# Fetching a and b from ScalarE's own queue, with their constants planned from the first microseconds

## The chip, the core and the metric

The kernel runs on one core of a Trainium2 chip. A core has a matrix engine (TensorE, PE in the rows; its weight loads are PEld), a vector engine (VectorE, DVE), an engine for activations and copies (ScalarE, ACT), a general engine (GpSimd, POOL) and SyncE (SP), which here only issues DMAs. Each engine works through its own queue in order and waits on semaphores for the others. The metric is the device time of one execution in microseconds; lower is better. The notation x4 at the end of a row means four instructions.

## The reference, cut to what matters

```python
def sm_attn(qq, kk, vv):
    s = scale * np.matmul(qq, kk.transpose(0, 1, 3, 2))
    s = s - np.max(s, axis=-1, keepdims=True)
    a = np.exp(s)
    a = a / (np.sum(a, axis=-1, keepdims=True) + 1e-09)
    return np.matmul(a, vv)
p_packed = sm_attn(p, k, v)              # 32 packed queries
x = sm_attn(q, p_packed, p_packed)       # 8 batches, 8 heads, 576 tokens, 64 per head
...
h = x @ w_in                             # 4608 x 512 by 512 x 2048
P = a[0] + a[1] * h + a[2] * h2 + a[3] * h3      # h2 = h * h, h3 = h2 * h
Q = 1.0 + np.abs(b[0]) * np.abs(h) + np.abs(b[1]) * h2
return (P / (Q + 1e-6)) @ w_out          # 2048 x 512
```

q, k, v and p are float32; the weights, a and b come as the kernel's inputs in DRAM. a has four numbers and b two.

## The kernel before, in words

The eight batches are worked on one after the other. For a batch, `attention` loads keys, values and queries in their natural layout, transposes them (the first batches on TensorE with a copy by ScalarE into the tile KX), and makes the packed attention: scores of p against k, an exponential, the product with v, normalised on VectorE into pT and transposed into PPT. The second attention follows: scores of PPT against the queries, transposed by VectorE back into KX, then a softmax over 32 keys in two halves (maximum, subtraction, exponential on ScalarE, sum, a reciprocal, a product), and a last transpose of each half into AH (and a rest AL from the second batch on). A softmax half thus goes VectorE, ScalarE, VectorE, and TensorE's hidden matmuls wait for both halves of AH.

The FFN is cut into units: a batch, one half of its tokens, and one of eight column blocks of w_in. Per batch `m_chunk` multiplies the packed values into w_in (tile m), so `hidden` of a unit is a matmul of AH with m into the PSUM tile h. Then come U (ScalarE, the absolute value times b0), sq (ScalarE, the square times b1's root), Y (ScalarE, a3*h + a2), two VectorE steps, a sum on GpSimd, a logarithm and an exponential in place of the division, and VectorE steps that leave the unit's result in gh and gl, and its remainder rows in G. These last steps read the unit's h for the last time; there are two h tiles, so the matmuls of a unit wait for the end of the unit two before it. Three units later `acc_block` multiplies gh and gl by w_out into the PSUM tile acc. Weights come as 64-bit words and are turned into float32 by `convert`: two ScalarE passes per block and three or four steps on VectorE or GpSimd; blocks of w_in and w_out wait for that in the tiles m, w, half.

Nearly all instructions are only recorded by `Planner`. It prices each, works out the dependencies, tries several list schedules, and issues the instructions in the order of the best one's start times (`issue`, line 293 for all instructions that it issues, so the tiles tell them apart). The planner's own DMAs all go to SP's queue. Where the plan leaves TensorE idle in the first 150 us, `idle` puts filler matmuls (line 290: columns of zeros added to an open PSUM sum, which change nothing) into the gap. The first instructions, before `nc.pin()`, are DMAs whose order is fixed.

The constants are made by `constants`, which is recorded right after the pinned DMAs: two DMAs bring a and b to all 128 partitions (tile ab); VectorE scales them into abS; a chain of VectorE steps, a logarithm and an exponential on ScalarE, and three more VectorE steps make the square root of b1 in the tile root and write it to abS. ScalarE then loads a3, b0 and the root into registers (TENSOR_LOAD rows) for its activations U, sq and Y. In the plan these steps come ready when ab's DMAs do.

Of the kernel before, what the change touches and what calls it, by code (L numbers as in the profile page):

```python
# [13 lines left out]
F32 = mybir.dt.float32  # L14
# [10 lines left out]
P = 128  # L25
# [7 lines left out]
class Planner:  # L33
# [8 lines left out]
    TRANSPOSE, F32 = (15, 0.734), (30, 1.62)  # L42
# [19 lines left out]
    SWITCH = 95  # L62
    SLACK = 60, 100, 150, 220, 300
    IN_FLIGHT = 8
    DMA_ISSUE, DMA_START, DMA_END = 420, 1400, 1200

    DMA_RATE = 100.0, 190.0, 370.0
# [90 lines left out]
    def edges(self):  # L158
# [32 lines left out]
            edges.append(before)  # L191
        return edges

    def schedule(self, before, after, rank, back=0):

        n = len(rank)
        need = [len(x) for x in before]
        at, start, end = [0.0] * n, [0.0] * n, [0.0] * n
        soon = {e: [] for e in self.ENGINES}
        ready = {e: [] for e in self.ENGINES}  # L200
# [2 lines left out]
        mode, landed, dma = None, [], 0.0  # L203
        for i in range(n):
            if not need[i]:
                heapq.heappush(soon[self.ops[i][0]], (0.0, rank[i], i))
        now = 0.0
        left = n
        while left:
            for e in self.ENGINES:  # L210
                while soon[e] and soon[e][0][0] <= now:
                    heapq.heappush(ready[e], heapq.heappop(soon[e])[1:])
                if free[e] > now or not ready[e]:
                    continue
                if e == "sync" and not back and len(landed) >= self.IN_FLIGHT and landed[-self.IN_FLIGHT] > now:
                    free[e] = landed[-self.IN_FLIGHT]
                    continue
                _, i = heapq.heappop(ready[e])
# [106 lines left out]
def attention_rational_ffn(  # L325
# [38 lines left out]

    sb = ctx.enter_context(tc.tile_pool(name="sb", bufs=1))
    ps = ctx.enter_context(tc.tile_pool(name="ps", bufs=1, space=PSUM))
    tc.nc.scalar.preload_act_table_set("natural_log_exp_and_others")
    nc = Planner(tc.nc)


    ident = sb.tile([P, P], F32, name="ident")
    make_identity(tc.nc, ident)
    ab, abS, one, root = (sb.tile([P, n], F32, name=x) for n, x in ((8, "ab"), (7, "abS"), (1, "one"), (5, "root")))
    ab, eps, minus = ab[:, 0:6], ab[:, 6:7], ab[:, 7:8]
    zero = sb.tile([P, 32], F32R, name="zero")
    win = sb.tile([P, NCH, NCC, CF], F32, name="win")
    G = sb.tile([P, NFC, 2 * REM], F32, name="G")
# [25 lines left out]
    def constants():  # L403
        nc.gpsimd.memset(eps, 1e-9)
        nc.gpsimd.memset(minus, -SCALE)
        nc.vector.tensor_scalar(zero, ident[:, 0:32], 0.0, None, ALU.mult)
        nc.sync.dma_start(ab[:, 0:4], a.rearrange("(o n) -> o n", o=1).broadcast_to([P, 4]))
        nc.sync.dma_start(ab[:, 4:6], b.rearrange("(o n) -> o n", o=1).broadcast_to([P, 2]))
        nc.vector.tensor_scalar(abS[:, 0:6], ab, S, None, ALU.mult)
        nc.vector.scalar_tensor_tensor(abS[:, 4:6], abS[:, 4:6], -1.0, abS[:, 4:6], ALU.mult, ALU.max)  # L410
        nc.vector.memset(one, (1.0 + 1e-6) * S)

        m, e, p, r, i = (root[:, n : n + 1] for n in range(5))
        nc.vector.scalar_tensor_tensor(m, ab[:, 5:6], -1.0, ab[:, 5:6], ALU.mult, ALU.max)
        nc.vector.tensor_scalar(m, m, 2.0**-126, None, ALU.max)
        nc.vector.tensor_scalar(e.bitcast(I32), m.bitcast(I32), 23, None, ALU.logical_shift_right)
        nc.vector.tensor_scalar(e.bitcast(I32), e.bitcast(I32), 127, None, ALU.add)
        nc.vector.tensor_scalar(p.bitcast(I32), e.bitcast(I32), 1, 23, ALU.logical_shift_right, ALU.logical_shift_left)
        nc.vector.reciprocal(i, p)
        nc.vector.tensor_scalar(m, m, i, i, ALU.mult, ALU.mult)  # L420
        nc.scalar.activation(r, m, AF.Ln)
        nc.scalar.activation(r, r, AF.Exp, scale=0.5)
        nc.vector.reciprocal(i, r)
        nc.vector.scalar_tensor_tensor(r, m, i, r, ALU.mult, ALU.add)
        nc.vector.tensor_scalar(abS[:, 6:7], r, p, 0.5 * S**0.5, ALU.mult, ALU.mult)
        for i, reg in enumerate((reg_a3, reg_b0, reg_b1, reg_root)):
            nc.scalar.reg_load(reg, abS[0:1, 3 + i : 4 + i].bitcast(I32))
# [576 lines left out]
    for what in ("k0", "k1", "r", "p", "qr", 2, "rv", "v0", "v1", 3, "q0", "q1", 4, 5):  # L1004
        if isinstance(what, int):
            load_words(what)
        else:
            load(0, what)
    nc.pin()
    constants()  # L1010
    for _ in attention(0):
        pass
# [17 lines left out]
    for bb in range(1, B):  # L1030
        gen = attention(bb)
        at = [u for u in range(2 * UB * bb - 30, 2 * UB * bb - 3) if u not in mt]
# [89 lines left out]
```

## Time and profile before

| what | value |
|---|---|
| time, median of 3 runs (lowest to highest) | 765.78 us (765.69 to 766.87) |
| the profiled execution | 766.86 us, of which its span is 765.1 us |
| busy, share of the span: PE, DVE, ACT, POOL | 96%, 86%, 81%, 61% |
| mean granted clock of TensorE | 0.983 of 2.4 GHz |
| DMA, busy share of 16 engines, first four fortieths of the span | 0.9, 0.9, 0.9, 0.4 |

A busy time counts all of an instruction's span; matmuls are pipelined, and their ends are modelled. "Idle before" is the time in which an engine stood still ahead of an instruction, with what released it. The granted clock is TensorE's: 1.00 is 2.4 GHz, 0.50 is 1.2 GHz.

### The profile page before, as it was taken

How to read it: one execution, taken by the hardware profiler on the slowest of the kernel's cores; microseconds unless marked ns; L12 is line 12 of the kernel's file. 1: busy time of each engine (PE TensorE's matmuls, PEld its weight loads, DVE VectorE, ACT ScalarE, POOL GpSimd, SP SyncE). 2: the span in 40 equal slices, each digit the busy share in tenths (PEclk: the TensorE clock that was granted, in tenths of full speed). 3: DMA queues.
4: the chain of work that ended last, by engine and by line, in shares of the span. 5: the costliest groups of instructions: out<-in, count | busy, mean ns of one | idle time of the engine just before them, and what ended most of it. 6: DMA issues, size and time to landing. Idle time of an engine off the chain costs nothing.

```text
span 765.1 us, 14505 instructions
## 1 busy us (share of the span) xinstructions
PE 737.9 (96%) x5358; PEld 569.2 (74%) x5358; DVE 656.0 (86%) x1050; ACT 619.1 (81%) x1074; POOL 467.4 (61%) x457
## 2 busy tenths in 40 slices
PE   3689999999999999999999999999999999999997
PEld 2455645678788887778788887778788887778886
DVE  2789999898988889998998789998998889988773
ACT  6689986898786888888786888888786887887882
POOL 0026556987685566856685565955685655866672
PEclk8679999999999999999999999999999999999999
DMA  9994650203801128024701119222801016000001
GB/s 253 292 371 129 164 135 0 83 26 50 120 1 56 43 32 126 10 84 55 112 1 57 36 24 126 25 84 32 116 14 56 27 24 83 1 28 1 29 1 41
DMA packets 156630, 56.38 MB, mean 74 GB/s; under 512 B 126864, under 2 KB 145808, under 8 KB 156560
## 3 DMA queue, kind: packets, MB, share of 16 engines
q1 hardware_dynamic: 156560, 55.46, 32.8%
q8 instruction: 42, 0.69, 0.4%
q14 instruction: 28, 0.23, 0.1%
HBM read 46.01 MB, written 9.44 MB: 72 GB/s over the span
## 4 chain that ended last, share of the span: by engine, by line
PE 89%; DMA 4%; ACT 2%; DVE 2%; POOL 1%; SPq 1%; issue 1%; DVEq 0%; POOLq 0%; ACTq 0%
PE acc L293 46%; PE h L293 28%; PE at L293 15%; DMA m<-in_moe_w_in_dram 2%; PE acc L290 1%; DMA pn<-in_p_dram 1%; DVE Y L293 1%; SPq L293 1%; DMA AH<-in_k_dram 1%; ACT sq L293 0%; ACT U L293 0%; POOL U L293 0%; POOL gl L293 0%; ACT h L293 0%; ACT Y L293 0%
## 5 line engine op out<-in xcount | busy, mean ns | idle before, releaser
L293 POOL TENSOR_TENSOR U<-U,sq 128x576 f32<-128x576 f32 x128 | 185.3, 1448 | 140.9 <-ACT sq L293 135.7
L293 DVE SCALAR_TENSOR_TENSOR Y<-Y,abS,h 128x576 f32<-128x576 f32 x256 | 205.7, 804 | 55.0 <-ACT h L293 52.9
L293 PE MATMUL acc<-w,gh 128*128 128x512 f32 x736 | 240.8, 407 | 0.5 <-ACT half L293 0.5
L293 PE MATMUL h<-AH,m 128*128 128x288 f32 x1024 | 195.6, 315 | 1.7 <-DVE AH L293 1.0
L293 PEld LDWEIGHTS h<-AH,m 128*128 128x128 f32 x1024 | 159.2, 189 | 30.8 <-DVE Y L293 7.5
L293 POOL TENSOR_TENSOR gl<-Y,gh 128x512 fp32r<-128x512 f32 x116 | 150.2, 1296 | 31.2 <-POOL G L293 13.5
L293 PEld LDWEIGHTS acc<-w,gh 128*128 128x128 f32 x736 | 133.9, 188 | 45.6 <-issue 16.4
L293 PE MATMUL acc<-w,gl 128*128 128x512 f32 x384 | 150.6, 412 | 0.0
L293 ACT ACTIVATE sq<-U,one 128x576 f32<-128x576 f32 x128 | 101.1, 790 | 34.9 <-POOL U L293 34.7
L293 ACT ACTIVATE U<-h 128x576 f32<-128x576 f32 x128 | 83.3, 651 | 40.3 <-PE h L293 39.6
L293 DVE TENSOR_TENSOR Y<-Y,h 128x576 f32<-128x576 f32 x128 | 95.3, 745 | 16.0 <-ACT Y L293 15.7
L293 ACT ACTIVATE h<-sq 128x576 f32<-128x576 f32 x128 | 84.8, 663 | 21.6 <-DVE Y L293 20.0
L293 PE MATMUL h<-AL,m 128*128 128x288 f32 x448 | 97.0, 296 | 0.0
L293 ACT ACTIVATE Y<-h,abS 128x576 f32<-128x576 f32 x128 | 96.5, 754 | 0.0
L293 DVE SCALAR_TENSOR_TENSOR h<-U,h 128x576 f32<-128x576 f32 x128 | 95.9, 749 | 0.0
L293 PEld LDWEIGHTS acc<-w,gl 128*128 128x128 f32 x384 | 71.8, 188 | 22.9 <-issue 10.2
L293 DVE SCALAR_TENSOR_TENSOR Y<-h,Y 128x576 f32<-128x576 f32 x116 | 87.0, 750 | 1.9
L293 ACT CAST gh<-Y 128x512 fp32r<-128x512 f32 x116 | 73.0, 629 | 14.8 <-DVE Y L293 10.1
L293 ACT ACTIVATE sq<-h 128x576 f32<-128x576 f32 x128 | 83.5, 653 | 0.0
L293 PE MATMUL acc<-half,gh 128*128 128x512 f32 x240 | 78.2, 409 | 0.2 <-ACT gh L293 0.2
L293 PEld LDWEIGHTS h<-AL,m 128*128 128x128 f32 x448 | 71.9, 188 | 2.0 <-issue 1.4
L293 PEld LDWEIGHTS acc<-half,gh 128*128 128x128 f32 x240 | 43.9, 188 | 13.5 <-issue 5.1
(145 smaller groups left out, 904.3 us busy)
## 6 DMA issues: line engine op xcount, KB each, us to landing
w<-in_moe_w_out_dram SPq DMA_DIRECT2D x16, 512.0 KB, 5.1
out_dram<-half SPq DMA_DIRECT2D x15, 512.0 KB, 3.0
nat<-in_k_dram SPq DMA_DIRECT2D x48, 144.0 KB, 4.3
nat<-in_q_dram SPq DMA_DIRECT2D x48, 144.0 KB, 4.4
nat<-in_v_dram SPq DMA_DIRECT2D x24, 256.0 KB, 3.3
m<-in_moe_w_in_dram SPq DMA_DIRECT2D x10, 512.0 KB, 8.9
w<-in_moe_w_in_dram SPq DMA_DIRECT2D x6, 512.0 KB, 8.2
nat<-in_k_dram SPq DMA_DIRECT2D x4, 512.0 KB, 7.1
```

The costliest lines, as they stand in the source:

```text
L290: getattr(self.nc.tensor, name)(*args, **kwargs)
L293: getattr(getattr(self.nc, engine), name)(*args, **kwargs)
```

## The change

The two DMAs that bring a and b are issued from ScalarE's queue, ahead of the load of its activation table and outside the planner. The planner no longer sees a DMA that writes ab; instead an instruction that reads the tile ab and has no other dependency comes ready at 4500 ns of its schedule (`LANDED`), and not at 0. Only the forward schedule uses it. Everything behind is planned anew.

```diff
+    LANDED = 4500.0
...
+    def ready(self, calls):
+        return self.LANDED * any(isinstance(x, bass.AP) and x.tensor.name == "ab" for _, args, _ in calls for x in args)
...
             if not need[i]:
-                heapq.heappush(soon[self.ops[i][0]], (0.0, rank[i], i))
+                at[i] = 0.0 if back else self.ready(self.ops[i][1])
+                heapq.heappush(soon[self.ops[i][0]], (at[i], rank[i], i))
...
+    tc.nc.scalar.dma_start(ab[:, 0:4], a.rearrange("(o n) -> o n", o=1).broadcast_to([P, 4]))
+    tc.nc.scalar.dma_start(ab[:, 4:6], b.rearrange("(o n) -> o n", o=1).broadcast_to([P, 2]))
     tc.nc.scalar.preload_act_table_set("natural_log_exp_and_others")
...
-        nc.sync.dma_start(ab[:, 0:4], a.rearrange("(o n) -> o n", o=1).broadcast_to([P, 4]))
-        nc.sync.dma_start(ab[:, 4:6], b.rearrange("(o n) -> o n", o=1).broadcast_to([P, 2]))
```

The seven added lines move the lines behind them: 290 and 293 of before are 296 and 299 in the changed kernel.

ScalarE's first instructions, before:

```order
L1118 UNCONDITIONAL_BRANCH
L367 ACT_TABLE_LOAD
L293 COPY kx_1_87<-at_1_89 128x512
L293 COPY kx_1_87<-acc_1_90 128x512
L293 COPY kx_1_87<-acc_2_91 128x512
L293 COPY kx_1_87<-at_2_92 128x512
```

and in the changed kernel:

```order
L1124 UNCONDITIONAL_BRANCH
L375 DMA ab<-in_moe_a_dram 128x4
L376 DMA ab<-in_moe_b_dram 128x2
L377 ACT_TABLE_LOAD
L299 TENSOR_LOAD abS x2
L299 ACTIVATE root<-root 128x1 x2
L299 TENSOR_LOAD abS
L299 COPY kx_1_89<-at_1_91 128x512
L299 COPY kx_1_89<-acc_1_92 128x512
```

The first batch's copies of transposed keys (kx) now stand behind all constants; before, the constants stood some 40 rows later, between the copies into m.

VectorE in the first batch's second softmax, from the product of the first half to just ahead of the second transpose into AH, before (m_4 and win are a w_in block in conversion, w_3 and w_8 one of w_out):

```order
L293 TENSOR_TENSOR kx_1_87<-kx_1_87,small 128x576
L293 TENSOR_SCALAR root<-root 128x1
L293 STREAM_TRANSPOSE AH_3_114<-kx_1_87 128x576
L293 TENSOR_REDUCE small<-kx_1_87 128x18
L293 RECIPROCAL root<-root 128x1
L293 TENSOR_SCALAR m_4_85<-m_4_85 128x1024
L293 TENSOR_SCALAR small<-small,ab 128x18
L293 SCALAR_TENSOR_TENSOR root<-root 128x1
L293 RECIPROCAL small<-small 128x18
L293 ISA win<-m_4_85,win 128x2048
L293 TENSOR_TENSOR kx_1_87<-kx_1_87,small 128x576
L293 TENSOR_SCALAR abS<-root 128x1
```

and in the changed kernel, from the conversion of that w_in block on:

```order
L299 TENSOR_SCALAR m_4_87<-m_4_87 128x1024
L299 RECIPROCAL small<-small 128x18
L299 ISA win<-m_4_87,win 128x2048
L299 TENSOR_REDUCE small<-kx_1_89 128x18
L299 TENSOR_TENSOR kx_1_89<-kx_1_89,small 128x576
L299 TENSOR_SCALAR small<-small,ab 128x18
L299 STREAM_TRANSPOSE AH_3_116<-kx_1_89 128x576
L299 RECIPROCAL small<-small 128x18
L299 TENSOR_SCALAR w_8_134<-w_3_88 128x1024
L299 TENSOR_TENSOR kx_1_89<-kx_1_89,small 128x576
L299 TENSOR_SCALAR w_3_88<-w_3_88 128x1024
L299 STREAM_TRANSPOSE AH_3_116<-kx_1_89 128x576
```

The steps on root and abS are gone from here; the w_in block's conversion has moved ahead of the first transpose into AH, and two steps of a w_out block ahead of the second.

TensorE around the hidden matmuls of the seventh unit (h_7), before (rows with zero are fillers; at_34 with small is the packed values' transpose):

```order
L293 MATMUL at_35_195<-rv_2_110,small 32x64
L290 MATMUL acc_14_167<-half_1_157,zero 32x96 x14
L293 MATMUL at_34_194<-ident,small 128x128
L290 MATMUL acc_14_167<-half_1_157,zero 32x96 x2
L293 MATMUL h_7_190<-AH_3_114,m_7_134 128x288 x4
L293 MATMUL at_34_194<-ident,small 128x128
L290 MATMUL acc_14_167<-half_1_157,zero 32x96 x6
L293 MATMUL h_8_204<-AH_3_114,m_7_134 128x288
```

and in the changed kernel:

```order
L299 MATMUL acc_14_169<-half_1_159,gh_2_173 128x512
L296 MATMUL acc_14_169<-half_1_159,zero 32x96 x5
L299 MATMUL at_38_211<-ident,nat_7_198 128x128 x3
L299 MATMUL h_7_192<-AH_3_116,m_7_136 128x288 x4
L299 MATMUL at_38_211<-ident,nat_7_198 128x128
L299 MATMUL acc_13_168<-half_2_180,gl_2_183 128x512 x2
L299 MATMUL acc_14_169<-half_2_180,gl_2_183 128x512
L299 MATMUL h_8_206<-AH_3_116,m_7_136 128x288 x4
```

The packed values of the second batch have moved ahead of h_7, query transposes and output matmuls of the fourth unit stand around it, and of 22 fillers five are left. Over the whole kernel the order lists 41 fillers of 96 columns before, and 30 of 96 and three of 256 columns after. The last 70 or so rows of TensorE, VectorE, ScalarE and GpSimd stand in the same order in both kernels, as do the last 54 DMAs of SP's queue.

## Rows read from the trace of the kernel before

**Rows 1.** The page, busy times: engine, us (share of span) x instructions.

```profile
PE 737.9 (96%) x5358; PEld 569.2 (74%) x5358; DVE 656.0 (86%) x1050; ACT 619.1 (81%) x1074; POOL 467.4 (61%) x457
```

**Rows 2.** The page, chain that ended last: shares by engine.

```profile
PE 89%; DMA 4%; ACT 2%; DVE 2%; POOL 1%; SPq 1%; issue 1%; DVEq 0%; POOLq 0%; ACTq 0%
```

**Rows 3.** Windows: stretch, length; busy us by engine; clock, DMA share, GB/s.

```profile
38.25:42.25 4.00, 4.00 (x8) 2.72 (x9) 4.00 (x10) 0.40 (x4) 0.00 (x0) 0.50 1.00 381
60.00:84.00 24.00, 24.00 (x222) 15.48 (x221) 23.90 (x47) 23.80 (x39) 11.31 (x6) 1.00 0.43 136
150.00:600.00 450.00, 449.50 (x3398) 359.12 (x3397) 401.40 (x634) 371.11 (x653) 300.76 (x302) 1.00 0.32 57
```

**Rows 4.** Timeline, the first 10 us: start, us, instruction [idle before <- releaser].

```profile
0.73 0.98 SPq L293 DMA_DIRECT2D nat<-in_k_dram  x2
0.73 1.28 ACT L367 ACT_TABLE_LOAD   x1 [0.73 <-PEq L1107]
...
4.83 1.08 PE L293 MATMUL at<-ident,nat 128*128 128x128 f32 x4 [4.83 <-DMA nat<-in_k_dram]
...
5.95 0.58 ACT L293 COPY kx<-at 128x512 f32<-128x512 f32 x1 [3.93 <-PE at L293]
...
9.10 0.37 ACT L293 COPY small<-acc 128x256 f32<-128x256 f32 x1
```

**Rows 5.** Timeline, 20 to 24 us.

```profile
20.89 1.92 PE L293 MATMUL acc<-w,kx 128*32 128x64 f32 x60 [0.97 <-DMA w<-in_v_dram]
22.21 1.05 SPq L293 DMA_DIRECT2D ab<-in_moe_b_dram  x1
...
23.59 0.33 SPq L293 DMA_DIRECT2D ab<-in_moe_a_dram  x1
23.66 1.15 ACT L293 ACTIVATE m<-m 128x1024 f32<-128x1024 f32 x1 [4.28 <-DMA m<-in_moe_w_in_dram]
```

**Rows 6.** DMA: the queue (packets, MB, share of 16 engines), issues (KB, us to landing).

```profile
q1 hardware_dynamic: 156560, 55.46, 32.8%
...
out_dram<-full SPq DMA_DIRECT2D x16, 64.0 KB, 1.7
...
ab<-in_moe_b_dram SPq DMA_DIRECT2D x1, 1.0 KB, 10.4
```

**Rows 7.** Timeline, 38 to 45 us.

```profile
38.25 4.21 PE L293 MATMUL h<-AH,m 128*128 128x288 f32 x8 [0.96 <-DVE AH L293]
...
41.59 0.21 DVE L293 TENSOR_SCALAR abS<-root 128x1 f32<-128x1 f32 x1
41.71 0.77 DVE L293 STREAM_TRANSPOSE AH<-kx 128x576 f32<-128x576 f32 x1
...
42.23 1.19 ACT L293 ACTIVATE w<-w 128x1024 f32<-128x1024 f32 x1 [3.60 <-DVE abS L293]
...
42.41 1.47 DVE L293 TENSOR_SCALAR w<-w 128x1024 uint16<-128x1024 uint16 x2
...
43.91 1.22 DVE L293 CUSTOM_DVE_ANT_0 w<-w,w 128x2048 uint16<-128x2048 uint16 x1
...
44.47 0.65 ACT L293 ACTIVATE U<-h 128x576 f32<-128x576 f32 x1
```

**Rows 8.** Timeline, 48 to 85 us, and one group of the page (busy, mean ns).

```profile
48.98 1.98 PE L293 MATMUL at<-ident,nat 128*128 128x128 f32 x8 [2.98 <-ACT m L293]
...
65.56 0.68 PE L290 MATMUL acc<-w,zero 128*32 128x96 f32 x6
...
66.17 2.21 PE L293 MATMUL h<-AH,m 128*128 128x288 f32 x8
...
79.61 2.22 ACT L293 ACTIVATE w<-w 128x1024 f32<-128x1024 f32 x2
...
82.27 0.67 DVE L293 SCALAR_TENSOR_TENSOR gl<-h,Y 128x512 f32<-128x512 f32 x1
...
84.03 0.72 ACT L293 ACTIVATE U<-h 128x576 f32<-128x576 f32 x1
...
L293 PE MATMUL acc<-w,gh 128*128 128x512 f32 x736 | 240.8, 407 | 0.5 <-ACT half L293 0.5
```

More of the change, by code (lines that the diff above doesn't have):

```diff
@@ L366, in attention_rational_ffn @@
     ps = ctx.enter_context(tc.tile_pool(name="ps", bufs=1, space=PSUM))
+    ab, abS, one, root = (sb.tile([P, n], F32, name=x) for n, x in ((8, "ab"), (7, "abS"), (1, "one"), (5, "root")))
+    ab, eps, minus = ab[:, 0:6], ab[:, 6:7], ab[:, 7:8]
+    tc.nc.scalar.dma_start(ab[:, 0:4], a.rearrange("(o n) -> o n", o=1).broadcast_to([P, 4]))
+    tc.nc.scalar.dma_start(ab[:, 4:6], b.rearrange("(o n) -> o n", o=1).broadcast_to([P, 2]))
     tc.nc.scalar.preload_act_table_set("natural_log_exp_and_others")
@@ L372, in attention_rational_ffn @@
     make_identity(tc.nc, ident)
-    ab, abS, one, root = (sb.tile([P, n], F32, name=x) for n, x in ((8, "ab"), (7, "abS"), (1, "one"), (5, "root")))
-    ab, eps, minus = ab[:, 0:6], ab[:, 6:7], ab[:, 7:8]
     zero = sb.tile([P, 32], F32R, name="zero")
```

## The prediction

> **What bounds the kernel now.** I read the busy times and the chain of waits first. TensorE is busy 737.9 of 765.1 us [rows 1], and 89% of the chain that ended last is TensorE's [rows 2]. By windows it loses 0.5 us between 150 and 600 us [rows 3], so the end is set by when the gap-free stretch begins, by the real matmuls that are left, and by the filler matmuls that stand among them. For this kernel I write: span = real matmuls + fillers + idle TensorE. The reals are the same in both kernels, so only two terms can move: the fillers, and the idle time, which is 765.1 - 737.9 = 27.2 us and lies nearly all before 55 us. What holds TensorE there is read from the timeline: first DMA (it starts on the first keys at 4.83 us, and waits for the values at 20.89 us; ScalarE waits 4.28 us for a block of w_in until 23.66 us [rows 4, 5]), then VectorE's softmax, which ends in the two transposes into AH, then ScalarE and VectorE together (23.8 and 23.9 of 24 us busy from 60 to 84 us [rows 3]).
>
> **The fetch.** Two issues leave SP's queue at 22.21 and 23.59 us (1.05 and 0.33 us [rows 5]) and stand ahead of the table load on ScalarE, which took 1.28 us from 0.73 us [rows 4]. At SP's own durations the table load ends at 0.73 + 1.38 + 1.28 = 3.4 us, before ScalarE's first copy at 5.95 us: cost 0. The transfers are 256 tiny packets. SP's queue moved 156560 packets in 32.8% of 16 engines' 765.1 us [rows 6], 0.41 us of all engines for 256. Until 22 us the DMA engines were the limit, so the values, the w_in blocks and the queries land later by 0 to 0.4 us; I take 0.4. Afterwards those packets are gone from the queue, but ScalarE and VectorE have already been set back, so I keep it as a shift.
>
> The Trainium skill ("DMA: Bandwidth & Descriptors", section "Issuing engines are not separate DMA queues") says that DMAs started by any engine run on the same 16 DMA engines, and another issuer saves only the time to issue. That speaks against the change: by it the 0.4 us is only moved, and 1.4 us of SP's issue time is the whole gain of the fetch. If ScalarE's queue had engines of its own, the 0.4 would be 0. No row of before has two issuers.
>
> **The constants at the head.** The order pieces on ScalarE show it: three register loads and two activations now stand in front of the first copy, and the order lists VectorE's twelve small operations likewise in front of its first reduction. So the copy at 5.95 us [rows 4] waits for a and b. Their landing is not in this trace for an empty queue: the quickest transfer took 1.7 us, this one in the full queue 10.4 us [rows 6], the first keys, issued at the same time, 4.83 - 0.73 = 4.1 us [rows 4]. I take 4.1, near the row with the same moment: landed at 0.8 + 4.1 = 4.9 us (bounds 2.5 and 11.2). Then twelve dependent steps (seven on VectorE, two activations, three on VectorE) at 0.21 us, the row of the last one [rows 7], are 2.5 us, and after that last one ScalarE went on 42.23 - 41.80 = 0.43 us later [rows 7]: ready at 7.8 us. The first copy comes 1.9 us late. The four copies ran with gaps; packed at 0.58 us [rows 4] the fifth, of the packed queries' projections, starts at 7.8 + 4 x 0.58 = 10.1 instead of 9.10 us [rows 4]. That is 1.0 us late, and hidden: ScalarE next idles 4.28 us until 23.66 us, and TensorE waits for the values until 20.89 us [rows 5]. Cost 0; the cover is gone when a and b land 3.3 us later still, after about 8.2 us.
>
> The register loads: after the last constant ScalarE lost 0.43 us with the load in it [rows 7]. The Trainium skill (same page, section "Latency and other measured facts") gives a tensor_load a floor of about 0.6 us; three in series would make the constants ready some 1.4 us later, which the same idle time still hides.
>
> **The stall that goes.** ScalarE waited 3.60 us for the last constant until 42.23 us [rows 7]. Behind that wait stood one weight conversion and two copies, done by the time U of the first unit started at 44.47 us, and U's matmuls set that start (TensorE ran at a granted clock of 0.50, 1.2 GHz, from 38.25 to 42.25 us [rows 3]). In the new order ScalarE has nothing more in front of that U, so it will wait for TensorE instead: worth 0 by itself.
>
> **VectorE's softmax (the order pieces on VectorE).** Eleven small operations leave the stretch; the last one moved its successor by 41.71 - 41.59 = 0.12 us [rows 7]; at 0.1 us each, 1.1 us is saved. But the two passes over a w_out block (1.47 us [rows 7]) now stand ahead of the second transpose into AH, and the conversion of a w_in block ahead of the first. Net, the second AH comes 1.5 - 1.1 = 0.4 us later, and the first about 2 us later, while four plus four transposes on TensorE go ahead of the hidden matmuls. Those took 4.21 us at half clock [rows 7]; if the clock returns as early as before, nothing is lost, if it returns 2 us later, 1.1 us. So U of the first unit shifts by 0.4 (DMA) + 0 to 1.1; I take 0.9 in all. From there ScalarE's queue is full, and the shift is handed on: idle TensorE +0.9 us.
>
> **Fillers.** The order lists 41 filler matmuls of 96 columns before; after, 30, and three of 256 columns. The three at 65.56 us, six instructions in the trace, took 66.17 - 65.56 = 0.61 us [rows 8], 0.20 each: -2.2 us. The wide ones lie between 0 and half of a 512-column one (0.41 us [rows 8]); 0.1 each: +0.3. Sum -1.9 us. It is a gain only if TensorE has real work ready there. One place speaks for it: before the seventh unit two conversions (2.22 us [rows 8]) have moved behind that unit's U, and two short copies in front, and the 22 fillers around the seventh unit's matmuls have become five (the order pieces on TensorE).
>
> **Sum.** -1.9 + 0.9 = -1.0 us. The profiled execution took 766.86 us (1.8 around its span), so 765.9 for it; the median of the runs shown is 1.1 lower, 765.78, so 764.8.
>
> **Rivals.**
> - *Full gain*: the clock returns early, U comes no later, and the 2.98 us for which TensorE waited until 48.98 us [rows 8] shrink by about half, since the copy it waited for moved ahead of two activations. -1.9 - 1.5 = -3.4, 762.4 us. Against it: the matmuls that follow need constants of other engines at 52 us as before. Chance 0.25.
> - *Nothing moves*: the fillers only stood in time that stays idle, and the shift is made up. 765.8 us, 0.1.
> - *VectorE becomes the bound at the eighth unit* (slower): in the new order a w_out block's two passes less one (0.74 us) and its last step (1.22 us [rows 7]) stand ahead of the gl that ends at 82.27 + 0.67 us [rows 8], on an engine 23.9 of 24 us busy [rows 3]. gl and its small partner are the last readers of the PSUM buffer that the eighth unit's matmuls take. +2.0 on top of the 0.9: TensorE idle +2.9 instead of +0.9, sum +1.0, and up to +2.0 if the fillers come back as idle time; 767.3 us. It decides when that buffer comes free after TensorE's own work ahead. Against it: 2.7 us of real matmuls have moved in front of that place. Chance 0.15.
> - *a and b land late* (slower): at 10.4 us, as in SP's queue, they are there at 11.2 and the fifth copy 7.3 us late, 3.0 beyond the 4.28: 764.8 + 3.0 = 767.8 us. Against it: nothing stands ahead of them in ScalarE's queue. The Trainium skill (same page, section "Queues, rings and completion order") says that each DMA engine takes turns between the queues; by that they don't wait behind the keys. Chance 0.1.
>
> **How the numbers follow.** The forecast case, 764.8, has 0.4 and spans 763.3 to 766.3 (its 0 to 1.5 of shift, fillers -1.5 to -2.2). About 0.2% is what a measurement of this kernel tells from no change, 1.5 us. Faster by more than that: a third of the forecast case, nearly all of the full gain: 0.13 + 0.24 = 0.38 with a little of "nothing moves". Slower: 0.02 of the forecast case, two thirds of the VectorE case, most of the late landing: 0.02 + 0.1 + 0.09 = 0.21. Within: 0.41. The range for 8 in 10 reaches to the full gain below and to the late landing above: 762.0 to 768.0.
>
> **What would show it.** Right: ScalarE's first copy near 7.8 us and the fifth near 10; the ScalarE wait until 23.66 us shorter by about 1 us, the values' matmuls at 20.9 to 21.3 us; no wait of 3.6 us near 42 us but one on TensorE; the first U at 44.9 to 46 us; the seventh U earlier than 84.03 us [rows 8]; fewer fillers and less than 1 us of new waits behind 84 us. Wrong: a or b landing after 8 us, waits of TensorE on VectorE between 80 and 90 us, or new TensorE gaps after 150 us.

## The result: slower by 1%

The changed kernel takes 774.95 us (773.15 to 776.1), the kernel before, beside it, 766.33 (765.69 to 768.6): 1.010 times as long, with a 95% interval of 1.008 to 1.012. Its profiled execution took 773.15 us with a span of 771.1; TensorE's mean granted clock is 0.981. The forecast, 764.8 us, has the wrong sign.

First the page of the changed kernel, busy times and the chain that ended last, against [rows 1, 2].

```profile
PE 741.2 (96%) x5339; PEld 568.8 (74%) x5339; DVE 660.8 (86%) x1050; ACT 618.1 (80%) x1074; POOL 465.6 (60%) x457
...
PE 65%; DVE 12%; ACT 9%; issue 5%; DMA 4%; POOL 3%; SPq 1%; DVEq 0%; ACTq 0%; POOLq 0%
```

TensorE is as full as before, but the chain that sets the end is TensorE's for 65% instead of 89%: it now passes through VectorE, ScalarE and GpSimd. By the sum that the prediction used, idle TensorE grew from 27.2 to 771.1 - 741.2 = 29.9 us, and its busy time from 737.9 to 741.2 although fillers left.

Next the first 12 us of the changed kernel, the counterpart of [rows 4]: TensorE's first matmul, then ScalarE with its own DMA issues.

```profile
5.91 1.09 PE L299 MATMUL at<-ident,nat 128*128 128x128 f32 x4 [5.91 <-DMA nat<-in_k_dram]
```

```profile
0.73 0.43 ACTq L375 DMA_DIRECT2D ab<-in_moe_a_dram  x1
1.19 0.45 ACTq L376 DMA_DIRECT2D ab<-in_moe_b_dram  x1
1.67 1.28 ACT L377 ACT_TABLE_LOAD   x1 [1.67 <-PEq L1113]
7.87 0.44 ACT L299 ACTIVATE root<-root 128x1 f32<-128x1 f32 x2 [4.92 <-DVE root L299]
9.39 0.58 ACT L299 COPY kx<-at 128x512 f32<-128x512 f32 x1 [1.08 <-PE acc L299]
...
11.30 0.42 ACT L299 COPY small<-acc 128x256 f32<-128x256 f32 x1
```

And its DMA queues with the landing times of ab (last column), against [rows 6].

```profile
q1 hardware_dynamic: 156272, 55.46, 34.0%
...
q10 hardware_dynamic: 288, 0.00, 0.0%
...
ab<-in_moe_a_dram ACTq DMA_DIRECT2D x1, 2.0 KB, 3.6
ab<-in_moe_b_dram ACTq DMA_DIRECT2D x1, 1.0 KB, 5.2
```

The keys land at 5.91 instead of 4.83 us. The second of the two fetches lands 1.19 + 5.2 = 6.4 us after the start, and VectorE's first constant follows it; the copies come 3.4 us later than before, and the fifth 2.2. ScalarE around the first U, against [rows 5, 7]:

```profile
24.41 1.15 ACT L299 ACTIVATE m<-m 128x1024 f32<-128x1024 f32 x1 [2.38 <-DMA m<-in_moe_w_in_dram]
...
42.95 1.19 ACT L299 ACTIVATE w<-w 128x1024 f32<-128x1024 f32 x1 [3.91 <-DMA w<-in_moe_w_out_dram]
...
44.96 0.66 ACT L299 ACTIVATE U<-h 128x576 f32<-128x576 f32 x1
```

The 4.28 us of idle time at 24 us shrank to 2.38, so the late copies were hidden, as forecast. The stall of 3.60 us is gone, and a wait of 3.91 us for a block of w_out stands at its place. The first U starts 44.96 - 44.47 = 0.49 us late. So far nothing has happened that would make 6 us. That comes behind it: the third U starts 1.6 us late (57.57 against 56.01), the fourth 4.2 (62.98 against 58.75), the eighth 1.8, the 24th 6.0. TensorE in that stretch in the changed kernel:

```profile
48.19 0.66 PE L299 MATMUL at<-ident,nat 128*128 128x128 f32 x4 [1.79 <-ACT m L299]
50.33 1.12 PE L299 MATMUL at<-ident,nat 128*128 128x128 f32 x4 [1.48 <-ACT m L299]
...
53.29 1.11 PE L299 MATMUL at<-kx,small 64*32 64x256 f32 x16 [0.46 <-ACT small L299]
54.33 3.20 PE L299 MATMUL h<-AH,m 128*128 128x288 f32 x8
```

and the third unit's hidden matmuls and those scores before:

```profile
53.45 2.10 PE L293 MATMUL h<-AH,m 128*128 128x288 f32 x8
55.48 0.66 PE L293 MATMUL at<-kx,small 64*32 64x256 f32 x16
```

Scores of the second batch's packed attention (at<-kx,small) stand ahead of the third unit's hidden matmuls, where before they stood behind, and the eight hidden matmuls take 3.20 us where they took 2.10. Windows of the changed kernel (columns as in [rows 3]):

```profile
50.00:55.00 5.00, 4.21 (x28) 2.62 (x29) 4.40 (x9) 4.95 (x9) 0.00 (x0) 0.50 1.06 325
55.00:60.00 5.00, 5.00 (x24) 3.26 (x23) 4.10 (x7) 3.17 (x5) 1.16 (x1) 0.86 1.06 348
60.00:84.00 24.00, 22.63 (x198) 12.45 (x197) 23.00 (x44) 22.66 (x40) 9.52 (x7) 1.00 0.38 120
150.00:600.00 450.00, 447.92 (x3364) 357.81 (x3364) 403.75 (x638) 368.73 (x650) 301.83 (x303) 1.00 0.35 57
```

and the first two of these stretches before:

```profile
50.00:55.00 5.00, 4.97 (x19) 3.67 (x20) 4.32 (x8) 4.88 (x9) 0.00 (x0) 0.72 1.04 391
55.00:60.00 5.00, 5.00 (x39) 2.70 (x38) 3.62 (x9) 5.00 (x9) 3.77 (x2) 1.00 0.91 263
```

Behind its gaps at 48 and 50 us TensorE had a granted clock of 0.50, the lower of its two levels (1.2 GHz), from 50 to 55 us, where before it was 0.72. From 60 to 84 us it lost 1.4 us where it had lost nothing, and from 150 to 600 us 2.1 us against 0.5 [rows 3].

A late U is not yet a loss, since the new order puts other work between the units. A better count is TensorE's real work: every matmul that is no filler counts with the mean time that its kind took in before at the full clock, and the question is how much later the changed kernel has done as much as before. This is an estimate worked out from the two traces, good to about 0.5 us; e1, below, comes out at 0.8 to 1.2 us late from 45 to 740 us. The changed kernel is 0.4 us late at 45 us, 3.8 at 65, 0.3 at 85, 0.5 at 105, 3.8 at 153 and 6.4 at 700. So what the opening loses is won back by 85 us, and the loss that stays comes behind 105 us. The fillers have a part in both. From 60 to 92 and from 113 to 150 us (PE busy, PEld busy, clock, DMA share, GB/s), before:

```profile
60.00:92.00 32.00, 6.24 (x62) 4.95 (x62) 1.00 0.49 144
113.00:150.00 37.00, 1.84 (x20) 1.62 (x20) 1.00 0.10 29
```

and in the changed kernel:

```profile
60.00:92.00 32.00, 2.03 (x20) 1.59 (x20) 1.00 0.44 138
113.00:150.00 37.00, 3.86 (x40) 3.22 (x40) 1.00 0.07 19
```

4.2 us of fillers have left the first stretch, and 2.0 us have come into the second.

One sentence of the text on the change has to be corrected. It says that an instruction that reads the tile ab comes ready at 4500 ns. The changed kernel compares the tensor's name with "ab", and the real name carries a number behind it, so the comparison never holds and the planner believes the constants ready at 0. That is why they stand ahead of all key copies (e3, below).

### The profile page after: what moved, and what is told of

The parts are those of the page before. It is cut to its first block, busy times and chain, and to the rows that moved or that the text cites. A ratio compares the mean times of both kernels' runs of the same rounds, so it can differ in the third digit from the quotient of the medians.

```text
span 771.1 us, 14483 instructions
## 1 busy us (share of the span) xinstructions
PE 741.2 (96%) x5339; PEld 568.8 (74%) x5339; DVE 660.8 (86%) x1050; ACT 618.1 (80%) x1074; POOL 465.6 (60%) x457
## 4 chain that ended last, share of the span: by engine, by line
PE 65%; DVE 12%; ACT 9%; issue 5%; DMA 4%; POOL 3%; SPq 1%; DVEq 0%; ACTq 0%; POOLq 0%
PE acc L299 33%; PE h L299 20%; PE at L299 12%; DVE Y L299 6%; DMA AH<-in_k_dram 3%; ACT sq L299 2%; DVE small L299 2%; DVE h L299 2%; DVE kx L299 2%; ACT kx L299 1%; ACT h L299 1%; POOL U L299 1%; ACT U L299 1%; SPq L299 1%; DMA w<-in_q_dram 1%
## 5 line engine op out<-in xcount | busy, mean ns | idle before, releaser
L299 PEld LDWEIGHTS acc<-w,gh 128*128 128x128 f32 x736 | 134.0, 188 | 49.4 <-issue 16.3
```

Of the source, the lines that this page charges most:

```text
L299: getattr(getattr(self.nc, engine), name)(*args, **kwargs)
```

## The experiments

Three kinds of edit were used. In the first, a kernel makes both plans, the one of before (its two DMAs of ab planned on SP's queue but not issued) and the one of the changed kernel, and issues a mixture, with the fetch at ScalarE's head. `HYBRID` names the plan that leads, until which of its starts it does, and the plan that orders the rest; `HOIST` puts the constants in front:

```diff
+HYBRID = ("old", 1e12, "old")
+HOIST = False
...
+        head = [i for i in order if start[i] < until and not self.fetches(i)]
+        if HOIST:
+            head = [i for i in self.constants if not self.fetches(i)] + [i for i in head if i not in self.constants]
+        done = set(head)
+        tail = [i for i in plans[rest][0] if i not in done and not self.fetches(i)]
```

In the second, a price of the planner changes by 1 to 5 ns, which means nothing to the chip but gives another order. In the third, the readiness of ab is changed. Three kernels add a small edit of their own. In the table "U1" is the start of the first U against 44.47 us before, "behind it" is the span's difference to 765.1 us less that, so it holds what happens after the first unit. U1 itself varies from one execution to the next: the changed kernel, e4, e6, e7 and e8 have the same ScalarE order up to there, and theirs lies between +0.49 and +3.70. So this column says more than one profile's span; the ratio comes from the timed runs.

| kernel | time, us | ratio to before (95%) | U1, us | behind it, us |
|---|---|---|---|---|
| the changed kernel | 774.95 | 1.008 to 1.012 | +0.49 | +5.5 |
| e1_fetch_only | 768.5 | 1.0014 to 1.0038 | +0.86 | -0.1 |
| e2_hoist | 768.31 | 1.0007 to 1.003 | +3.36 | +0.7 |
| d1_fetch_twice | 769.41 | 1.0019 to 1.0053 | +2.56 | +0.6 |
| n1_fetch_later | 776.23 | 1.0101 to 1.0142 | +7.47 | +0.8 |
| e3_seen | 774.85 | 1.0091 to 1.0121 | +0.83 | +6.6 |
| e4_lead_new | 773.82 | 1.0078 to 1.0106 | +3.70 | +3.2 |
| e5_lead_old | 776.7 | 1.0106 to 1.0146 | +2.59 | +7.4 |
| e6_until_48 | 771.01 | 1.0041 to 1.0075 | +1.27 | +2.6 |
| e7_until_62 | 774.94 | 1.0088 to 1.0124 | +1.79 | +6.2 |
| e8_port | 773.48 | 1.0059 to 1.0102 | +1.04 | +5.4 |
| l1_switch_96 | 771.86 | 1.0037 to 1.0084 | +0.07 | +5.4 |
| l2_switch_90 | 767.45 | 1.0003 to 1.0025 | -1.39 | +0.4 |
| a_switch_90 | 775.15 | 1.0081 to 1.0148 | +0.44 | +7.0 |
| a_switch_94 | 776.95 | 1.0081 to 1.0186 | +2.94 | +7.0 |
| a_switch_97 | 774.22 | 1.0071 to 1.0139 | +3.33 | +5.1 |
| a_switch_100 | 776.65 | 1.01 to 1.0162 | +3.40 | +6.4 |
| s_seen_15000 | 770.21 | 1.0021 to 1.0054 | +3.03 | +0.5 |
| s_seen_36000 | 785.32 | 1.0199 to 1.0267 | +22.2 | -3.9 |

**The fetch alone** (e1_fetch_only): before's order, only the two DMAs at ScalarE's head.

> Only the fetch moves: a and b from ScalarE's queue at the head, every other instruction in the order of before, constants at their old place. Theory 'order' (the new order of the first units on ScalarE, VectorE and TensorE costs the time): the keys land about 1 us later, the idle time until 24 us hides most of it; 0 to +1 us against before (766 to 767.3). Theory 'head' (a late start is handed down to the end): part of the loss is here already, +2 to +4 us.

Every U stands 0.75 to 0.86 us late, the first as much as the last, and nothing is added behind. TensorE's first matmul in this run:

```profile
6.62 1.09 PE L330 MATMUL at<-ident,nat 128*128 128x128 f32 x4 [6.62 <-DMA nat<-in_k_dram]
```

In the four kernels without a fetch at the head (before, l1, l2, n1) this start is 4.79 to 4.92 us; in all others 5.91 to 6.88. So the fetch sets the first keys back by 1 to 2 us. Its packets do not do this by filling the DMA engines. From 2.5 to 4.5 us (columns as in [rows 3]) before, and then in e1:

```profile
2.50:4.50 2.00, 0.00 (x0) 0.00 (x0) 0.00 (x0) 0.00 (x0) 0.00 (x0) 1.00 0.96 321
```

```profile
2.50:4.50 2.00, 0.00 (x0) 0.00 (x0) 0.00 (x0) 0.55 (x1) 0.00 (x0) 1.00 0.47 119
```

The DMA engines' share is 0.91 to 0.96 in the four kernels and 0.40 to 0.57 in the sixteen with the fetch, so the engines ran emptier. The fetch's own packets took 1.7% of 16 engines' first 8 us in the changed kernel, 0.14 us. Why the keys came late is open. By the profile the fetch costs 0.8 us in the end, by the timed runs 0.14 to 0.38%, 1.1 to 2.9 us. The median of 768.5 us lies above the range of "order" and, 1.9 us over the 766.6 beside it, just short of that of "head": by the timed runs about a quarter of the loss may be the fetch's.

**The constants in front as well** (e2_hoist; `HOIST = True`).

> The fetch and the constants at the head, as in the changed kernel, everything else in the order of before. Theory 'order': -1 to +1 us against before (the 3.6 us stall goes, the first U comes about 0.5 us later). Theory 'head': near the changed kernel, +6 to +9 us, since ScalarE's first copy comes at 9.4 us as there.

Its interval overlaps that of e1. Its profiled execution, with a late first unit (47.83 us), was the slowest of eleven, 771.02 us; the median is 768.31. The early constants by themselves cost and bring nothing that these runs can tell apart, and "head" falls.

**The fetch doubled** (d1_fetch_twice): e1, and the same two DMAs once more into a tile that is still unused.

```diff
+    spare = G[:, NFC - 1, :]
+    tc.nc.scalar.dma_start(spare[:, 0:4], a.rearrange("(o n) -> o n", o=1).broadcast_to([P, 4]))
+    tc.nc.scalar.dma_start(spare[:, 4:6], b.rearrange("(o n) -> o n", o=1).broadcast_to([P, 2]))
```

> The order of before, the fetch from ScalarE's queue at the head, and the same two DMAs once more behind it (into columns of the tile G that are written later). In the fetch-only run the first unit came 0.86 us late and the end 0.8. If the tiny packets are what delays the keys: the first keys another 0.8 to 1.1 us later (6.7 to 7.0 us), the first unit and the end another 0.5 to 0.9 us: 768.5 to 770. If it is only that a second queue takes part: keys at 5.9 us, 768 to 768.7.

The first matmul starts at 6.36 us, no later than with one fetch and earlier than the 6.7 to 7.0 expected from the packets; the median is 0.9 us above e1's, with overlapping intervals. So twice the packets do not set the keys back further. What one packet costs stays open.

**The fetch later** (n1_fetch_later): before's order, the two DMAs issued from ScalarE's queue ahead of its first conversion of a w_in block, near 14 us.

```diff
+            if engine == "scalar" and calls[0][0] == "activation" and calls[0][1][0].tensor.name.startswith("m0_1_"):
+                for j in self.constants:
+                    if self.fetches(j):
+                        _, args, _ = self.ops[j][1][0]
+                        self.nc.scalar.dma_start(*args)
```

> The order of before, a and b fetched from ScalarE's queue at about 14 us, behind the first exponentials, when the keys have landed. SP's two issues go as in the change. If the 0.8 us of the fetch-only run came from the keys and what is queued behind them: 766 to 767, no different from before. If the packets cost the same wherever they are put in front of the values and the w_in blocks: 767 to 768.

Missed, and by much. ScalarE in this run:

```profile
14.68 0.24 ACT L335 ACTIVATE small<-small 128x4 f32<-128x4 f32 x1
19.91 0.38 ACTq L333 DMA_DIRECT2D ab<-in_moe_a_dram  x1
22.79 0.33 ACTq L333 DMA_DIRECT2D ab<-in_moe_b_dram  x1
23.17 1.10 ACT L335 ACTIVATE m<-m 128x1024 f32<-128x1024 f32 x1 [8.25 <-DMA w<-in_q_dram]
```

Between the end of an activation at 14.92 us and its next instruction at 23.17 ScalarE stood still, and the two issues are the only instructions in between: the first appears 5 us after ScalarE was free, the second 2.5 us after the first. The releaser named in the last row is a transfer that the activation does not need, but the second issue waited for it. The chain of waits shows this (start, us, what):

```profile
14.19 8.57 DMA w<-in_q_dram
22.76 0.02 issue
22.79 0.33 ACTq L333
```

The trace has the semaphores too. In before, the changed kernel, e1, d1, l1 and n1 the DMAs of both queues take one of eight semaphores in turn, and an issue waits until the transfer that had its semaphore before has landed. Here the first issue waited for a block of w_in, issued by SP at 11.66 us and landed at 19.89, and the second for a block of queries, landed at 22.76. At the head of ScalarE's queue all eight are free. The first unit came 7.5 us late, and everything behind it too, although the keys came on time (first matmul at 4.90 us). So the run says nothing on the packets' price. The head of the queue is the better place for a fetch by ScalarE; it is not free there.

**The readiness seen** (e3_seen): the changed kernel with a name test that holds, so that LANDED has its effect.

```diff
-        return self.LANDED * any(isinstance(x, bass.AP) and x.tensor.name == "ab" for _, args, _ in calls for x in args)
+        return self.LANDED * any(isinstance(x, bass.AP) and x.tensor.name.startswith("ab_") for _, args, _ in calls for x in args)
```

> The changed kernel with its test for the tile ab mended (the tile's real name ends in a number, so the test never held and the planner took the constants as ready at 0): the planner now sees them at 4500 ns. ScalarE's keys are copied between the constants; nothing else differs from the changed kernel's order. Theory 'order': within 1 us of the changed kernel (774 to 775.5). Theory 'head': most of the loss goes, 767 to 769.

The key copies now stand among the constants, the order behind the first batch's head is that of the changed kernel, and so is the time. The copies that come 3.4 us late are not the cause.

**Half of one order, half of the other**: `HYBRID = ("new", 100e3, "old")` (e4), `("old", 100e3, "new")` with HOIST (e5), `("new", 48e3, "old")` (e6) and `("new", 62e3, "old")` (e7), where the number is a time in the plan in ns.

> The changed kernel's order up to 100 us of its plan, the order of before for all the rest. Theory 'order', early units: the loss of 4.3 us that the unit starts show by the 27th unit stays, and the 1.5 to 2 us lost after 200 us go: 770.5 to 772.5. If the loss lies in the later order: 766 to 768. Theory 'head' does not tell here: 770 to 773.

> The mirror of the kernel that led with the new order: fetch and constants at the head, the order of before up to 100 us of its plan, the changed kernel's order for the rest. If the early order carries the loss: 768 to 769.5, as with the old order throughout (768.3) or up to 1 us more. If the late order carries as much: 771 or more.

> The changed kernel's order only up to 48 us of its plan (the head, the softmax with the w_in block moved ahead of AH, the first two units' activations), the order of before for the rest. If the softmax's order or the head were the loss, as in the prediction's shift of 0.9 us: 769 to 770 at most. Theory 'second attention early' (the second batch's scores and exponentials, planned ahead of the third to sixth units, cost the time): 768 to 769, no more than the old order with the constants at the head.

> The same with the seam at 62 us of the plan, behind the fourth unit and the second batch's scores and exponentials. Theory 'second attention early': the larger part of the 6 us is here, 771.5 to 774. If the loss is spread over all units: 769.5 to 771.

All four are slower than e1. e4, e6 and e7 end above every range that was given for them (773.82, 771.01 and 774.94 us); e5, at 776.7, meets "771 or more", the late order carrying as much. A mixture has waits of its own where the plans meet, so the sizes can't be read as shares. By the count of real work e4, its late first unit (+3.70) included, is 2.2 us late at 105 us and 7.1 at 116: its loss arises at the seam and says nothing on the opening. e6 and e7 are about 4 and 8 us late from 75 us on and lose nothing behind that; they lost it up to and at their seams. e5 is 3.3 us late at 105 us, 7.1 at 125, 7.5 at 153 and 10.4 at 700: behind a good opening the changed kernel's later order loses again, a part of it at the seam. From 150 to 600 us TensorE's idle time goes with the later order: 2.0 to 2.1 us in the changed kernel, e3, e5 and e8, 0.5 in before, e1, e4, e6 and e7.

**One wait taken away** (e8_port). In the changed kernel ScalarE waits about 1 us twice for a tiny VectorE step that takes 1.4 us:

```profile
58.85 1.42 DVE L299 TENSOR_SCALAR small<-small,ab 128x2 f32<-128x2 f32 x1
...
64.95 1.37 DVE L299 TENSOR_SCALAR small<-small,ab 128x2 f32<-128x2 f32 x1
```

```profile
60.30 0.47 ACT L299 ACTIVATE kx<-at,small 128x256 f32<-128x256 f32 x1 [0.92 <-DVE small L299]
...
66.42 0.47 ACT L299 ACTIVATE kx<-at,small 128x256 f32<-128x256 f32 x1 [1.03 <-DVE small L299]
```

In e8 the step takes another form, without the column of ab.

```diff
+                if name == "tensor_scalar" and isinstance(args[2], bass.AP) and args[2].offset % 8 == 7 and args[2].tensor.name.startswith("ab_"):
+                    name, args = "scalar_tensor_tensor", (args[0], args[1], -1.125, args[1], ALU.mult, ALU.add)
```

> The changed kernel's order unchanged; four small VectorE operations (the product of a maximum with a constant from the tile ab, 128x2) are done as another instruction, a maximum times -1.125 plus itself. In the changed kernel two of them took 1.42 and 1.37 us instead of 0.22 while GpSimd was at work, and ScalarE waited 0.92 and 1.03 us behind them. If that hold-up is handed down: 772 to 773.5 against 774.9. If other waits take its place: 774.5 to 775.

The first of the two steps took 0.16 us, the second still 1.37. The fourth U came 1 us nearer to the third (4.39 us behind it against 5.41), but by the end nothing of it is left: +5.4 us behind the first unit against +5.5. The median of 773.48 us lies in the range for a hold-up that is handed down, but its interval overlaps that of the changed kernel, and the trace does not show a gain that lasts. Taking away one of the two waits paid for nothing that can be told apart.

**Meaningless new plans of the kernel before** (l1_switch_96, l2_switch_90): no fetch moved, one price changed.

```diff
-    SWITCH = 95
+    SWITCH = 96
```

> The kernel before, with nothing of the change; one price in the planner is 96 ns in place of 95 (a matmul after one of another shape). Work, tiles and the fetch are those of before; the new plan moves some 390 rows of TensorE and 230 of VectorE, about as many as the change did. Theory 'any new plan': the chosen order of before is a lucky one, and a new plan costs 3 to 10 us whatever caused it: 769 to 776. Rival 'the constants at the head are what the plan stumbles over': within 2 us of before.

> The same with 90 ns: another new plan of the unchanged work. Theory 'any new plan': 769 to 776 again, at another value. Rival: within 2 us of before.

A price of 1 ns costs 5.4 us behind the first unit, one of 5 ns 0.4. The first of them is worth a look. Its ScalarE order is row for row that of the changed kernel from the first U to behind the fifth, 45 rows, though its constants stand about where they stood before. Its rows show the same events at nearly the same times:

```profile
53.91 3.59 PE L293 MATMUL h<-AH,m 128*128 128x288 f32 x8
```

```profile
58.82 1.42 DVE L293 TENSOR_SCALAR small<-small,ab 128x2 f32<-128x2 f32 x1
...
64.92 1.37 DVE L293 TENSOR_SCALAR small<-small,ab 128x2 f32<-128x2 f32 x1
```

```profile
57.53 0.65 ACT L293 ACTIVATE U<-h 128x576 f32<-128x576 f32 x1 [1.60 <-PE h L293]
...
62.95 0.66 ACT L293 ACTIVATE U<-h 128x576 f32<-128x576 f32 x1
```

and its windows of 50 to 55 and of 150 to 600 us:

```profile
50.00:55.00 5.00, 4.54 (x28) 2.83 (x29) 4.40 (x8) 4.95 (x9) 0.00 (x0) 0.50 1.03 376
...
150.00:600.00 450.00, 446.85 (x3358) 356.74 (x3357) 403.74 (x634) 366.45 (x645) 298.91 (x301) 1.00 0.33 57
```

Its third and fourth U stand at 57.53 and 62.95 us, the changed kernel's at 57.57 and 62.98. So this opening does not need early constants, nor the fetch. But it is not what costs the 5.4 us. By the count of real work l1 is 4.0 us late at 65 us and 0.4 at 85, like the changed kernel, then 0.7 at 200 us and 5.7 at 740: it loses behind 200 us. l2 is 4.2 us ahead of before at 105 us, with 17 fillers in place of 82, and has lost 3.6 of it at 740.

**Meaningless new plans of the changed kernel** (a_switch_90, 94, 97, 100): the changed kernel with SWITCH at these values.

> The changed kernel whole (its fetch, its early constants, its readiness rule), with the planner's price SWITCH at 90 instead of 95, so that only a tie-breaking cost of 5 ns differs and everything is planned anew. Theory 'draw' (the fetch costs about 0.8 us, the rest of the loss is the luck of this one plan): plans of the changed kernel scatter over some 766.5 to 775 us, and some of the four redrawn plans end near 767 to 769. Theory 'structure' (constants that are free from the first microseconds make every plan pull the second batch's first attention ahead of units 3 to 6 and lose there): all four end at 772 or more. Here: draw 767 to 772, structure 772 to 777.

> The changed kernel with SWITCH at 94. Draw: 767 to 774, not predictable for one plan. Structure: 772 to 777.

> The changed kernel with SWITCH at 97. Draw: 767 to 774, not predictable for one plan. Structure: 772 to 777.

> The changed kernel with SWITCH at 100. Draw: 767 to 774, not predictable for one plan. Structure: 772 to 777. If one of the four lies below 765.5, it beats both kernels.

The theory of the single unlucky draw falls: with the changed kernel itself, five plans lie between 774.2 and 777 us, all 5.1 to 7.0 us behind the first unit. In all five, TensorE stands at a clock of 0.50 for one of the 5 us windows between 50 and 60 us, and the fourth U starts 3.7 to 5.4 us behind the third; in before, e1 and l2 that distance is 1.7 to 2.8 us. That is a mark that they share, not the place of the loss: by the count of real work the five lose 5.2 to 7.4 us between 105 and 740 us. TensorE's idle time from 150 to 600 us is 4.2 to 5.8 us in the four new plans, against 0.5 in before; in a_switch_90:

```profile
150.00:600.00 450.00, 444.19 (x3356) 354.49 (x3355) 403.37 (x634) 368.76 (x645) 299.88 (x300) 1.00 0.31 57
```

**The constants planned later** (s_seen_15000, s_seen_36000): the fetch at ScalarE's head, the test mended as in e3, LANDED at 15000 and 36000.

```diff
-    LANDED = 4500.0
+    LANDED = 15000.0
```

> The changed kernel with the name test mended and LANDED at 15000, so that the fetch stays on ScalarE's queue but the planner puts the constants behind the first batch's first attention (among the conversions of the first w_in blocks), where they are ready long before they are needed. Theory 'early constants' (constants in the first microseconds of the plan draw the second attention and everything behind it into a worse order): this plan is closer to that of before and ends at 766.5 to 770 us (before plus 0.8 for the fetch, plus or minus the luck of one plan). Theory 'fetch out of the plan' (any plan without the two DMAs is worse): 773 to 777. Theory 'draw of a tuned plan' (any plan but the one of before ends some 1 to 10 us later, whatever the constants): 768 to 777.

> The same with LANDED at 36000: the constants stand still later in ScalarE's order, about where they stood before. Early constants: 766.5 to 770. Fetch out of the plan: 773 to 777. Draw of a tuned plan: 768 to 777.

The first comes out at 770.21 us, just above the range of "early constants" and within that of "draw of a tuned plan", and is only 0.5 us slower behind its first unit. But the edit did more than was meant: a column of the tile ab holds a scale that the packed softmax reads, and the instruction that fills this column came ready late too. ScalarE's first exponential stands at 20.59 us instead of 11.76, and the first U 3.0 us late; with 36000 the first U stands at 66.66 us. So the second kernel says nothing on the question, and the first only that a plan with the fetch out of SP's queue need not lose 5 us behind the first unit (by the count of real work it is 4.5 us late at 105 us and 4.0 at 740). TensorE's clock was 0.50 in both windows from 50 to 60 us there too, so that sign alone does not decide either; the fourth U stands 1.9 us behind the third. None of these kernels is faster than before.

## Why the prediction was wrong, point by point

- *The bound.* "Span = reals + fillers + idle" held as a sum, but the claim that "only two terms can move" failed. Fillers fell from 82 instructions to 63 in the trace, 8.08 us of busy time to 6.56, so by 1.5 us and not 1.9, while TensorE's busy time rose by 3.3 us: the reals took 4.8 us longer. About 1.7 of this is more time at half clock before 92 us (9.8 us against 8.1 of busy time lost to the clock; the last such stretch ran from 49.6 to 56.4 us instead of 49.4 to 52.8). The rest is open.
- *The fetch, 0 to 0.4 us taken as 0.4.* Mis-sized, and the mechanism was another: the term priced the packets' time on full engines. Their own time (288 of them, not 256) was 0.14 us, the engines ran half empty, and still the keys came 1.08 us late; e1 hands on 0.8 us to the end. The Trainium skill ("DMA: Bandwidth & Descriptors", section "Issuing engines are not separate DMA queues") was weighed there: another issuer saves only the time to issue. This case agrees: the second issuer did not make the transfers free.
- *The constants at the head, cost 0.* Right, although they came later than said: b landed at 6.4 us and not at 4.9, so the first copy started at 9.39 us (forecast 7.8) and the fifth at 11.30 (10.1). The wait at 24 us fell from 4.28 to 2.38 us and hid it; e2 and e3 confirm it. The three register loads took 0.48, 0.29 and 0.28 us, two of them long before the last constant, so their price had no part in it.
- *The stall that goes, 0.* Right: 3.60 us gone, 3.91 of waiting for w_out at its place, no earlier U.
- *The softmax, first U +0.9 us.* It came 0.49 us late, inside the stated 0.4 to 1.5, which is in part luck: with the same opening it lay between 0.49 and 3.70 us. The two transposes into AH came 2.4 us and 0.8 us late (39.82 and 42.50 us), the forecast being 2 and 0.4.
- *Fillers -1.9 us, idle +0.9.* This is the step that failed: "the shift is handed on" held the new order behind the first U to be as good as the old. The gain of the fillers that left near the seventh unit was real, 4.2 us from 60 to 92 us, more than the whole term; but it only paid for what the opening had lost by 65 us. Then 43 of the 63 fillers that are left stand after 113 us, where before 20 of 82 did, and TensorE's idle time rose by 2.7 us, 1.6 of it between 150 and 600 us, where the prediction expected no gap and had named new gaps as a sign that it was wrong. From rows of the old order I could price what moved around the first U, not what an order of a thousand rows would do behind it.
- *Rivals.* "VectorE becomes the bound at the eighth unit" had the sign, but not the place: the eighth U is 1.8 us late, and by the count of real work TensorE has won back by then what it lost at the third and fourth unit; it loses again between 105 and 153 us (the 12th U 2.2 us late, the 16th 5.1). "a and b land late" was a tenth of the chance and did not happen. "Full gain" and "nothing moves" are refuted by the measured time; the clock came back later, and the wait of 2.98 us became two, of 1.79 and 1.48.

Shown: the fetch costs about 0.8 us in the profile (e1; 1.1 to 2.9 by the timed runs), the constants in front nothing that can be told apart (e2, e3), and all that is left, some 5.5 us, comes with the new order behind the first unit (the changed kernel against e1). By the count of real work, an estimate, this is the order behind 105 us and not the opening: l1 has the same opening on ScalarE and, like the changed kernel, has won it back by 85 us. Not shown: why the changed kernel's plans all come out like this. That its constants are free early would fit five plans of five, but l1 and l2, with constants as late as before, also lose 4.6 and 3.6 us behind 105 us, and the one test with late constants had a second effect in it. Of the three plans with before's fetch, before's own is the best behind 105 us; it may be an uncommonly good one. Nor is it settled which rows of the new order carry the loss from 105 us on.

## What to carry to other kernels

An edit to a planned kernel is two changes: what it does on the chip, and a new order of everything. Try them apart, with the old order and the edit alone (here 0.8 us in the profile), then the planner's order with a price changed by a nanosecond (here 0.4 to 5.4 us); a forecast from rows of the old order holds only as far as the order does. To find where an order loses, count what the engine at the limit has done by a given time; a unit that starts late may only have let other work pass. None of nine new orders tried here was faster than the old one, and an idle time removed at 42 us is worth nothing if no critical row stands behind it.

## What the runs showed of the hardware

- A fetch of 288 tiny packets from a second queue at the start set the first 512 KB of keys back: the first matmul on them starts at 5.91 to 6.88 us in 16 kernels instead of 4.79 to 4.92 in four. The packets' own time was 0.14 us of all engines, and these were emptier meanwhile (share 0.40 to 0.57 instead of 0.91 to 0.96); twice the packets (d1) set the keys back no further.
- A DMA issue in ScalarE's stream can cost more than the 0.4 us of its row. In n1 two of them held ScalarE for 8.25 us, each until the transfer that had its semaphore before had landed: landings at 19.89 and 22.76 us, issues at 19.91 and 22.79.
- A VectorE step on 128x2 elements took 0.14 to 0.3 us or 1.4. In the long cases a sum on GpSimd ran beside it and ended with it:

```profile
58.84 1.40 POOL L299 TENSOR_TENSOR U<-U,sq 128x576 f32<-128x576 f32 x1 [9.48 <-ACT sq L299]
...
64.90 1.40 POOL L299 TENSOR_TENSOR U<-U,sq 128x576 f32<-128x576 f32 x1 [2.29 <-ACT sq L299]
```

These end at 60.24 and 66.30 us, the two VectorE steps at 60.27 and 66.32. The Trainium skill ("SBUF — State Buffer", section "SBUF: two separate sides") has a pair of ports that VectorE in some of its forms and GpSimd take by an exclusive lock for a whole instruction; by that the small step waited for the sum, if it is of such a form. The traces of the changed kernel and e8 agree in three of four cases: in e8, in the other form, one of the two steps beside such a sum took 1.37 us, and the other, which began 0.01 us after its sum, 0.16.
